# A new order table for a recurrent-attention and gated-MLP kernel: pairs loaded in natural order, weights at other places

## The chip, the cores and the metric

The kernel runs on one core of one Trainium2 chip. The metric is the device time in microseconds (us) of one execution; lower is better. The engines are PE (matrix products; PEld loads its weights), DVE, ACT and POOL (elementwise work), and SP, which here only issues transfers between memory and the chip.

## The reference

Two steps, on float32 inputs with batch 4, 8 heads, 768 positions, head size 48, model width 384, and 1024 hidden columns:

```python
for t in range(S):                       # gated linear attention, per batch and head
    state = alpha[:, :, t, :, None] * state + outer(k[:, :, t], v[:, :, t])
    y[:, :, t] = q[:, :, t] @ state
x = y, heads side by side                # [4, 768, 384]
h = maximum(x @ w_in, 0)                 # [4, 768, 1024]
u, v = h[..., :512], h[..., 512:]
v_n = (v - mean(v)) / sqrt(var(v) + 1e-6)
v_s = w_spatial @ v_n + b_spatial[:, None]   # mixes positions, [768, 768]
out = (u * v_s) @ w_out                  # [4, 768, 384]
```

## The kernel before

The 768 positions of each batch are cut into six chunks of 128; the 24 chunks are numbered through. Chunks 0 to 9 are worked as five pairs (`pair(j)`), the other fourteen singly (`single(i)`).

For a pair or a chunk, the work runs like this. Four loads (`ac`, `kc`, `qc`, `vc`; 384 KB each for a pair, 192 KB for a chunk, named `acs` and so on). A logarithm of alpha (`ln`, ACT). Its running sums (`cum`, `tot`, PE). Exponentials of the sums with both signs (`einv`, `eexp`, `ebc`, ACT). Products that give the scaled keys and queries (`kt` on POOL or DVE, `qt` on DVE) and a bfloat16 copy of v (`vb`). Transposes on PE (`tr`, `trk`) whose two halves are copied out of the matrix banks into `kqT` by `ev` or `evs`, each on DVE or ACT. Scores (`sc`, PE), masked on DVE (`m`, `ms`). The state update (`upd` on PE, `z` on DVE, `S` on POOL or DVE, the bfloat16 copy `sb`). The output of the chunk (`ya`, `y`, PE) and its copy `xe` into xT.

For each batch follow the projections: `v` per chunk (three matmuls of 512 columns), its copy with a maximum (`ve`), statistics (`bn`), an inverse deviation (`rs`) and the normalised `vn`; `u` per quarter of the hidden columns and half of the positions (three matmuls of 384 columns, copy `ue`); the spatial mix `s` in two parts, the first over the chunks 0 to 3 and the second over 4 and 5, with `se` (adds the bias) and `g` (multiplies by u); the output `o`, its copy `oe` and its store `st`. The spatial weights come in three loads (`w_sp`), are cast, transposed on PE (`wt`) and copied (`we`). `w_in` comes in two loads, `w_out` in one; the six weight loads share two buffers (`raw`), so that a weight load waits for the casts of the one before the last.

The order of everything is written out by hand in the string `PLAN`. A word such as `P94@7` is operation 94, issued on PE, into bank 7; D is DVE, A is ACT, G is POOL, S is SP. The operation numbers come from the order in which the Python code creates the operations. `replay` goes through the words and issues one after the other, so the words of one letter are the order of that engine's queue, and each engine works its queue strictly in that order:

```python
        for x in junk:
            cols, n = x.split("#")
            ...
            warm(int(cols), int(n))
        ...
        op.emit(eng)
```

A word may carry junk: `:512#0` calls `warm` ahead of the operation, a float32 matmul of 512 columns on the tile `junk` into bank 0, whose result nobody reads. `junk` is filled by operation 0 (`zeros`, DVE).

Line numbers used below: 268 `warm`; 431 the loads of pairs; 796 the weight loads; 210, 212 the copies on ACT and the other engines; 216, 218 the copies with a maximum; 221 products of two operands; 384 `z`; 452, 460 running sums; 518, 696 transposes; 543, 712 updates; 561, 724 scores; 569, 729 masks; 584, 740 chunk outputs; 754 all projections; 816, 817 statistics; 833 `vn`; 889 `se`; 920 stores.

Of the kernel before, what the change touches and what calls it, by code (L numbers as in the profile page):

```python
# [41 lines left out]
S53 D2 S103 D0 G8 G4 A57 P59@0:512#0:512#0:184#0 A107 A62 P58@1 D3
P51@2 P108@3:100#3 S54 P109@4 D1 A63 A60 S55 G5 A114 A61 A64
S162 A110 P49@5 D50 G6 D68 D65 A111 D66 D69 A166 P71@6,7:384#6
P74@5,1:144#5 A72 S56 G70 S105 P167@0:100#0 S104 A67 D73 D52 A112 D75
P168@7 P77@2,5 D78 A76 A113 P84@6,1:76#6 S163 S164 A169 A171 S106 G79
D116 S268 D86 G118 A80 P87@2,3:88#2 D85 A170 D119 G115 D89 D88
P124@1,6:236#1 P121@4,3:164#4 D81 D122 P90@2,5:52#2 A126 A125 D123 G177 S165 A172 D174
# [8 lines left out]
G281 D160 D285 P216@0 D282 A153 P212@1 P201@6 D161 A19 A205 A149
P214@3 P34@4,2 G284 D206 D211 G21 A217 A213 A202 D35 S23 P31@7,0
D33 P290@1,5 D101 A36 A32 P37@6,4 A38 P287@2,0 D39 D203 D289 G286
P154@7 A283 A215 G22 S319 D288 A207 D208 S322 P226@4 P218@6 P293@3,0  # L60
D209 A292 D294 D291 A155 P40@2,5 A42 P227 S320 P219 P222@7 G24
P223 A25 G295 S321 P46@3,5 A41 D228 A47 D220 A323 D224 P43@1,4
P230@2 A45 D297 P300@6,7 G221 P303@3,0 G229 S379 G334 A44 D48 P325@5
P231 P324@4 P234@1 D301 P238@6 G298 D304 G225 D326 S26 P239 A331
A327 A329 P242@3 P243 P235 A330 D305 G332 A328 D232 P246@0 G335
D302 D336 S403 D244 D333 A337 D240 P247 G296 P338@2,7 A339 G299
P341@5,3 A340 D236 P306@4,6 A383 S405 P308 P344@1,2 D342 D343 G233 S380
G245 S404 A307 S381 S546 G28 P351@5,7 A309 A30 D248 P354@3,0 P310@4
S382 G27 P313@6 G29 D345 D352 G346 P384@1 D356 A407 A311 D353
P408@5 G237 D355 P256@0 A385 S406 A347 P250@4 A314 D312 S513 D315  # L70
S489 P357@7,3 P358 S547 A409 S548 S490 S492 A386 G249 A359 P360
A410 P253@6 D348 D412 D254 G411 G388 A251 P365@7 A361 P362@2 A316
P373@4 A363 D389 G241 P391@5,3 P414@6,2 D257 S515 A366 A550 S491 P369@0
A374 G349 S611 A416 D364 G390 A392 S514 A370 A387 S516 P371@7
P259@4 D393 A517 D415 S635 P394@3 P398@6,2 S570 P417@5,0 D375 P265@1 D395
P518@3 G413 S549 G396 D399 A260 P262@6 G397 D419 A493 D418 A519
P367@4 S636 D400 D318 P420@0 G350 P401@5 P494@2 A263 D421 A376 A266
P551@6 D317 A495 D402 P425@1 A520 P422@0 A426 D377 S571 P435@5 S572
D378 S612 A521 A552 A423 D368 P433@1 S613 A553 P439@4 G498 A372
S637 S573 D427 D424 A500 A428 A436 P447@0 P443@7 G555 D523 S721  # L80
S614 S638 A497 G522 P437@3 D429 A434 D430 P504@5 D556 A496 D505
G506 P444 P448 A554 D499 P440 A438 D449 D445 P451@1 P452 D453
G507 P501@6,5 A524 D502 D441 P558@3,2 P525@0,7 P459@1 D526 P460 A503 G446
D559 P528@6 P431@5 S722 P508@4,0 G454 A527 G450 D560 A432 D529 A574
P565@7,3 P532@2,6 D461 P455@5 D567 P575@1 G442 P467@3 G557 A615 S778 G530
S723 P468 D566 D533 P474@7 A639 S745 D509 A576 D510 D534 A577
P616@2 A531 P561@4 P456 D562 P463@0 P640@6 D580 A617 P464 D457 P477@4
D469 A475 G579 D465 A618 G620 A641 G643 P582@7,5 S724 A578 D621
A584 P511@1 D583 P568@3 A642 S746 P535@0 A512 A478 A619 P471@5 D644
P537@7 P589@1,4 D569 G462 S748 A536 D472 P646@6,2 A538 D590 A581 S747  # L90
P623@0,3 D539 D648 P540@5 A647 D625 G563 S843 A624 P594@7 G458 P603@1
P585@6 A725 D591 A541 A622 G466 A595 P649@0,2 D586 G564 G470 P630@3,5
S780 P592@4 A604 G587 P726@6 S802 P626@7 D650 D542 S779 A593 S867
P486@1 D632 A727 P605@0 P480@4 A728 S845 G588 A487 D627 P599@5 S781
A782 G645 D631 A481 G730 S844 A543 D731 D651 A729 P483@1 D596
A606 G628 P733@7,3 D607 S803 A749 S869 G629 P633@4 D544 P652@6 D732
A634 P783@2 A653 A600 A608 P601@0 P597@4 P654@6 P736@5 A484 P750@1 A734
A655 S804 D735 D610 A751 A752 A786 S868 P667@3 D545 P657@7 P663@6
G754 A658 D737 D609 A598 P671@5 D656 P699@7 D602 A784 D659 A668
A847 P683@0 P679@4 D756 S805 P760@3 A660 D662 D661 A664 D755 P675@6  # L100
G738 A785 P684 A806 S846 A753 S261 D761 P672 S252 D788 P665@3
P676 D673 P680 P700 G787 D685 G686 P790@1,2 A666 P740@5,3 D677 D681
A871 P757@0,6 P848@4 G762 A791 S258 D741 A758 D792 P687@1 A759 G763
A789 A851 P797@5,0 P764@2,6 D742 P695@3 D701 G674 P669@7 A849 D765 D799
G852 P688 G678 P807@2 S870 D798 P691@0 A850 P872@5 G682 D670 D766
P696 A808 P793@7 P692 P706@6 S479 A873 S482 A810 A739 A809 A874
S473 D794 D697 S488 P703@7 A707 P767@3 G811 D853 G795 A704 D812
P800@4 D876 P743@6 G875 A768 A801 P855@2,7 S705 D693 P814@5,3 D689 D856
A744 G813 P878@0,4 P769@6 P817@1 P772@2 A815 A816 D698 A879 P821@5,3 D880
G702 D818 A796 D857 P881@4,0 G854 G819 A770 S476 P862@1,7 D823 D864  # L110
D822 P835@6 A773 P858@3 G694 D882 P709@2 D859 A877 P831@7 G820 D863
P829@5 A836 A710 P826@4 D883 D771 G860 P833@6 A827 P824@2 G690 A861
D828 P865@3 A825 A866 P884@1 P837@4 D834 P886@0 D830 A885 D774 A838
P899@2 P897@3 S255 A775 P889@1 A887 P901@6 D839 D776 D777 A840 D832
D841 A890 P715@4 D842 P718@5 D891 A716 D888 P895@0 P903@7 D902 P712@1
P907@4 A900 P919@2 S708 A892 D894 P911@6 D898 D893 P904 P912 D905
D906 P915@3 S485 A713 P916 S267 P908 D917 D909 P927@1 G918 D913
P920 A719 A896 D910 P923@5 P924 P931@0 D914 P928 P932 D925 D921
D929 S717 D922 S720 P940@7 D933 P934@3 P937@4 G926 D930 A941 P946@6
P952@5 A947 S714 S711 D935 P943@2 P949@1 S264 D938 A944 A950 D953  # L120
# [871 lines left out]
```

## Time and profile before

| | |
|---|---|
| Median of 3 runs | 147.65 us (147.55 to 148.86) |
| Span of the profiled execution, first to last instruction | 145.2 us |
| Mean granted PE clock | 0.983 |
| PE busy | 135.1 us (93%), 2243 matmuls, 38 of them junk (12.7 us) |
| DVE busy | 123.5 us (85%) |
| ACT busy | 103.4 us (71%) |
| POOL busy | 79.7 us (55%) |
| Loaded and stored | 23.60 MB and 4.72 MB |

Of the profiled execution the profile gives the span, not the device time around it; the median of the runs is 2.45 us above the span. Busy time counts an instruction from its start to its end, and on PE neighbouring matmuls overlap and their ends are modelled, so a busy PE may still be waiting between operations. On ACT and DVE an instruction's record is about 0.1 us longer than the distance to the next start.

### The profile page before, as it was taken

The page shows a single profiled execution, that of the slowest core. Times are in us where ns is not written, and L with a number is a line of the kernel's source. Part 1 is how long each engine was busy: PE and PEld are TensorE (multiplying, and loading weights), DVE is VectorE, ACT ScalarE, POOL GpSimd, SP SyncE. Part 2 cuts the span into 40 slices and gives each one's busy share as a digit, 9 for nine tenths or more (in the row PEclk, how much of TensorE's full clock was granted, in tenths as well). Part 3 has the DMA queues.
Part 4 walks back from the last instruction along what each step waited for, and adds up shares of the span by engine and source line. Part 5 has one row for each costly group of instructions (what it writes and reads, how often), then busy time and mean ns, then how long its engine had stood idle before and what let it go on. Part 6 is the DMA issues. An engine that isn't in the chain of part 4 may idle for free.

```text
span 145.2 us, 5523 instructions
## 1 busy us (share of the span) xinstructions
PE 135.1 (93%) x2243; PEld 83.1 (57%) x2243; DVE 123.5 (85%) x284; ACT 103.4 (71%) x262; POOL 79.7 (55%) x120
## 2 busy tenths in 40 slices
PE   5979899489999999999999999999999999999990
PEld 2447576344565665656556665665666766555560
DVE  5047999577999999799999998999799999997970
ACT  3579627817997669899895889999876996653031
POOL 6301944559325999954549789644369984000500
PEclk9999999977999999999999999999999999999997
DMA  4999999995799999977989999999999990015045
GB/s 116 267 261 261 266 237 276 287 320 117 227 305 264 282 188 187 184 156 145 197 171 194 182 171 178 210 167 204 190 152 237 317 362 14 5 56 209 8 146 181
DMA packets 84841, 28.66 MB, mean 197 GB/s; under 512 B 79568, under 2 KB 83280, under 8 KB 84816
## 3 DMA queue, kind: packets, MB, share of 16 engines
q1 hardware_dynamic: 84784, 28.32, 88.0%
q8 instruction: 17, 0.28, 0.9%
q14 instruction: 8, 0.07, 0.2%
q0 software_dynamic: 32, 0.00, 0.0%
HBM read 23.60 MB, written 4.72 MB: 195 GB/s over the span
## 4 chain that ended last, share of the span: by engine, by line
PE 71%; DVE 21%; issue 5%; ACT 0%; ACTq 0%; DVEq 0%
PE bank L754 45%; PE bank L268 5%; DVE stats L816 3%; DVE ptm L569 3%; DVE vn L833 2%; DVE ptm L729 2%; DVE qt L221 2%; PE bank L696 2%; PE bank L724 2%; PE bank L406 2%; PE bank L663 2%; PE bank L452 2%; PE bank L584 2%; PE bank L740 2%; DVE kqT L212 1%
## 5 line engine op out<-in xcount | busy, mean ns | idle before, releaser
L754 PE MATMUL bank<-w_spT,vn 128*128 128x384 bf16 x192 | 35.6, 326 | 0.3 <-DVE vn L833 0.2
L221 POOL TENSOR_TENSOR gT<-vs,uT 128x384 bf16<-128x384 f32 x25 | 22.5, 914 | 16.8 <-DVE vs L889 16.8
L221 POOL TENSOR_TENSOR kt<-kc,binv 128x384 bf16<-128x384 f32 x21 | 19.3, 930 | 10.8 <-ACT binv L673 8.7
L754 PEld LDWEIGHTS <-vn 128*128 128x128 bf16 x192 | 17.7, 97 | 12.3 <-DVE vn L833 1.2
L221 POOL TENSOR_TENSOR state<-zs,bc 128x384 f32<-128x384 f32 x20 | 16.7, 834 | 14.0 <-DVE zs L384 10.4
L754 PE MATMUL bank<-w_in,xT 128*128 128x512 bf16 x72 | 19.8, 406 | 0.0
L754 PE MATMUL bank<-xT,w_in 128*128 128x384 bf16 x96 | 19.4, 326 | 0.0
L754 PE MATMUL bank<-w_out_sb,gT 128*128 128x384 bf16 (+1 forms) x100 | 18.4, 320 | 0.1
L729 DVE TENSOR_TENSOR ptm<-bank,mask 128x512 bf16<-128x512 f32 x28 | 17.9, 681 | 0.4 <-PE bank L724 0.4
L216 ACT ACTIVATE v_sb<-bank 128x512 bf16<-128x512 f32 x23 | 13.7, 609 | 5.4 <-PE bank L754 5.3
L816 DVE BATCH_NORM_STATS2 stats<-v_sb 128x6 f32<-128x512 bf16 x24 | 16.4, 682 | 1.3 <-ACT v_sb L216 0.8
L889 DVE TENSOR_TENSOR vs<-bank,bsp_bc 128x384 f32<-128x384 f32 x31 | 15.9, 548 | 1.0 <-PE bank L754 0.8
L268 PE MATMUL bank<-junk 128*128 128x512 f32 (+16 forms) x38 | 12.7, 429 | 2.5 <-DVE junk L311 1.8
L210 ACT COPY kqT<-bank 128x512 bf16<-128x512 bf16 x22 | 12.1, 603 | 3.3 <-PE bank L518 1.7
L221 DVE TENSOR_TENSOR qt<-qc,bank 128x384 bf16<-128x384 f32 x24 | 12.7, 545 | 0.8 <-ACT bank L675 0.8
L569 DVE TENSOR_TENSOR ptm<-bank,mask 128x512 bf16<-128x512 f32 x20 | 13.0, 682 | 0.2 <-PE bank L561 0.2
L754 PEld LDWEIGHTS <-gT 128*128 128x128 bf16 x100 | 9.2, 98 | 5.9 <-issue 0.3
L754 PEld LDWEIGHTS <-w_in 128*128 128x128 bf16 x96 | 8.8, 97 | 6.6
L216 ACT ACTIVATE uT<-bank 128x384 bf16<-128x384 f32 x22 | 10.7, 499 | 2.0 <-PE bank L754 2.0
L833 DVE TENSOR_SCALAR vn<-v_sb,mvs,rstd 128x512 bf16<-128x512 bf16 x24 | 10.6, 466 | 1.3 <-ACT rstd L827 1.1
L268 PEld LDWEIGHTS bank<-junk 128*128 128x128 f32 x38 | 6.6, 210 | 8.8 <-issue 5.2
L384 DVE TENSOR_TENSOR zs<-bank,state 128x384 f32<-128x384 f32 x16 | 8.8, 550 | 2.8 <-PE bank L543 2.5
(110 smaller groups left out, 251.7 us busy)
## 6 DMA issues: line engine op xcount, KB each, us to landing
ac<-in_alpha_dram SPq DMA_DIRECT2D x14, 192.0 KB, 4.8
qc<-in_q_dram SPq DMA_DIRECT2D x14, 192.0 KB, 4.8
kc<-in_k_dram SPq DMA_DIRECT2D x14, 192.0 KB, 5.0
vc<-in_v_dram SPq DMA_DIRECT2D x14, 192.0 KB, 4.4
raw_w<-in_moe_w_spatial_dram SPq DMA_DIRECT2D x3, 768.0 KB, 4.5
out_dram<-raw_w SPq DMA_DIRECT2D x11, 192.0 KB, 3.0
ac<-in_alpha_dram SPq DMA_DIRECT2D x5, 384.0 KB, 5.4
kc<-in_k_dram SPq DMA_DIRECT2D x5, 384.0 KB, 6.3
```

The lines of the kernel that those rows point to most:

```text
L210: nc.scalar.copy(out=out, in_=in_)
L216: nc.scalar.activation(out=out, in_=in_, func=AF.Relu)
L221: ENG[eng].tensor_tensor(out=out, in0=in0, in1=in1, op=ALU.mult)
L268: nc.tensor.matmul(out=banks[n][:, 0:cols].rearrange("p (a b) -> p a b", a=4), lhsT=junk, rhs=junk[:, None, 0:cols // 4].to_broadcast([128 ...
L384: nc.vector.tensor_tensor(out=zs[i % 3], in0=tp(), in1=state[(i - 1) % 3], op=ALU.add)
L406: nc.tensor.matmul(out=place(y, n) if q(hp).shape == place(y, n).shape else place(y, n).rearrange("p (a t) -> p a t", a=2), lhsT=sbd[(i - ...
L569: nc.vector.tensor_tensor(out=ptm[n2][:, par, s], in0=banks[sl.bank].rearrange("p (hp t) -> p hp t", hp=HP), in1=mask[:, par][:, None, :]. ...
L729: nc.vector.tensor_tensor(out=ptm[n2][:, ci, s], in0=banks[sl_p[s].bank].rearrange("p (hp t) -> p hp t", hp=HP), in1=mask[:, 2][:, None, : ...
L754: nc.tensor.matmul(out=ps, lhsT=lhsT, rhs=rhs, start=first and n == 0, stop=last and n == len(pairs) - 1)
L816: nc.vector.bn_stats(out=stats[tt % 2], in_=v_sb[n2][:, tt, :])
L833: nc.vector.tensor_scalar(out=vn[n2][:, x, :], in0=v_sb[n2][:, x, :], scalar1=mvs[n2][:, x, 0:1], scalar2=rstd[n2][:, x:x + 1], op0=ALU.su ...
L889: nc.vector.tensor_tensor(out=vs[d], in0=banks[sl.bank][:, 0:TH], in1=bsp_bc[:, th, :], op=ALU.add)
```

## The change

Only the string `PLAN` differs. All 955 operations, their inputs and outputs and the rules of what waits for what are the same. The new table moves nearly every operation on every queue, gives some operations to another engine, other banks to PE's results, and other junk.

The loads on SP stand like this (before, then after, up to the first single chunk):

```
ac_0 ac_1 kc_0 qc_0 ac_2 vc_0 qc_1 kc_1 kc_2 qc_2 vc_1 ac_3 vc_2 w_in_1 w_in_0 qc_3 w_sp_0 kc_3 w_sp_1 vc_3 w_sp_2 ac_4 vc_4 kc_4 qc_4 acs_10 w_out

ac_0 qc_0 vc_0 kc_0 ac_2 ac_1 vc_1 kc_1 qc_1 w_in_1 qc_2 kc_2 w_in_0 vc_2 w_sp_0 ac_3 w_sp_1 w_sp_2 ac_4 qc_3 kc_3 w_out qc_4 vc_3 kc_4 acs_10 vc_4
```

Operations that change engine, net, where it is more than one: `ev` and `evs` copies 16 from DVE to ACT; `ue` 4 and `oe` 2 from DVE to ACT; `g` 4 and `S` 3 from POOL to DVE; `ve` 2 from ACT to DVE; casts of weights 4 to DVE (three from POOL, one from ACT) and 3 from ACT to POOL; `sb` 3 to DVE, and `vb`, `vbs` 3 from ACT to POOL. Junk goes from 19 calls with 3340 columns, the last ahead of operation 97, to 9 calls with 3664 columns, the last ahead of operation 134.

The first third of both tables:

```diff
-S53 D2 S103 D0 G8 G4 A57 P59@0:512#0:512#0:184#0 A107 A62 P58@1 D3
-P51@2 P108@3:100#3 S54 P109@4 D1 A63 A60 S55 G5 A114 A61 A64
-S162 A110 P49@5 D50 G6 D68 D65 A111 D66 D69 A166 P71@6,7:384#6
-P74@5,1:144#5 A72 S56 G70 S105 P167@0:100#0 S104 A67 D73 D52 A112 D75
-P168@7 P77@2,5 D78 A76 A113 P84@6,1:76#6 S163 S164 A169 A171 S106 G79
-D116 S268 D86 G118 A80 P87@2,3:88#2 D85 A170 D119 G115 D89 D88
-P124@1,6:236#1 P121@4,3:164#4 D81 D122 P90@2,5:52#2 A126 A125 D123 G177 S165 A172 D174
-D178 P92 P137@6,1 G82 P134@4,3 G117 A91 G120 A173 D175 D138 D136
-P180@2,7:108#2 P183@0,6:112#0 D184 A272 P127@3,0:56#3 A185 D135 A179 A93 D128 D139 S9
-G129 D181 P273@4:136#4 P274@3 A83 D182 P193@1,6:104#1 G130 D131 P190@2,7 G132 D194
-S13 A176 P140@0,5:80#0 G7 D275 A11 A12 P143 P141 G10 A133 D195
-A276 D192 P186@1 S270 P97@6:192#6 S17 A144 D187 P94@7 G188 G16 P156@1
 ...
+S53 D0 G4 A57 P58@0:512#0:472#0 A60 D1 A61 G5 G8 S55 D2 G6 D66 P59@1 A62 A63 D69 P74@0,2:512#2:272#2 A76 D3 S56 D70
+S54 D75 P51@3 S162 G67 G68 D65 P71@2,0:360#4 A73 D72 P87@0,2:280#4 D89 A166 P167@4 P84@5,6 S103 P77@2,7 S106 S104 A64
+A107 P108@1 A110 A169 S105 D78 G120 G79 G7 D85 D88 D86 P109@2 A114 A111 A52 A112 A170 A113 G118 D115 P49@5
+P121@3,6:512#0:512#0 D81 A117 P127@7,0 D116 D119 D80 G82 S9 P124@2,1 A126 A122 A125 D128 D129 D131 P168@7 A171 A123
+A172 A173 P90@3,1 S164 S163 D175 P134@6,2:232#0 A91 G11 G12 D178 D135 D136 G10 G132 G174 G177 P92 P183@4,0 P137@3,7
+D138 D139 A93 G133 P94@1 A185 G83 A95 P97@2 S13 S165 P180@1,3 G16 A181 A182 P140@7,0 P141 A130 D184 D96 D15 D50
+P193@3,1 D194 D195 P190@4,6 G14 D192 D191 A142 A98 D99 G176 A179 P145@7 P143 A144 A146 S17 P186@1 P150@3 P156@6 P148@4
+G18 D187 D188 D157 A151 A100 D147 D158 D101 A19 S268 S20 G189 P196@3,7 P152@1 P197 P154@0 P199 A198 P201@3 D202 D102
+P31@6,2 A153 G21 G22 A200 P216@7 P34@1,5 P214@3 D36 P204@5 A33 D217 D203 S23 D35 S319 A155 A272 A159 A149 D161 D32
+D160 A205 P37@7,0 P212@2 A38 P273@1 P40@5,4 P274@6 A39 P226@0 P222@7 D206 G24 G25 D275 A276 A42 A213 A207 D208 P218@2
 ...
```

Some of the numbers: 57 to 64 logarithm, sums and exponentials of pair 0; 71, 74 the transposes `tr_k_0`, `tr_q_0`; 77 `upd_0`; 84, 87 its scores; 90 `ya_0`; 94, 97, 145, 156, 201, 204 the six `v` of batch 0; 121, 124, 134, 137 transposes and scores of pair 1; 122, 123, 125, 126 the `ev` copies of pair 1; 180, 183, 186 transposes and update of pair 2; 196 `ya_2`; 208, 209 the last `vn` of batch 0; 218 to 247 the `s` of batch 0; 31 to 46 `wt` and `we`; 9, 13 `w_in`; 17, 20, 23 `w_sp`; 26 `w_out`.

More of the change, by code (lines that the diff above doesn't have):

```diff
@@ L41 @@
 PLAN = """
[L42 to L48, printed above, removed]
@@ L57 @@
[L57 to L64, printed above, removed]
@@ L65 @@
[L65 to L120, printed above, removed]
@@ new lines @@
+D209 P223 D224 P219 D220 A277 A41 P46@5,4 S270 P227 D228 A323 A278 D282 P324@7 A215 A47 P43@3,2 A279 D285 D44 A48 A45
+P230@5 P325@1 P231 P210@2 A327 P290@3,4 A211 P246@0 P242@2 P247 S269 D281 D326 D284 D232 S26 S321 S271 D29 D292 P243
+P287@4,5 A291 A328 A329 A28 A331 G221 G229 G233 D30 G225 D27 D244 D333 P238@3 P239 P256@2 D248 A330 D336 D240 S320
+A289 A280 A288 P303@4,0 A257 A286 D304 P300@6,7 S379 G249 D302 D305 S322 P250@1 A251 P341@4,3 A342 A343 A383 G283
+P293@2,5 D294 D301 G332 D295 P234@1 P235 G335 P338@2,3 A340 G296 S403 D236 S381 S380 P306@6,0 P384@4 A339 P308 S382
@@ new lines @@
+S404 S405 D245 D297 P351@2,3 P354@1,7 D309 D352 D356 A385 A337 G241 A307 G334 P253@5 P344@6,0 P310@2 A254 A407 P408@7
+P313@5 G298 G299 A386 G237 D355 D345 D353 P262@6 G346 A409 P357@3,1 P358 D389 D347 P360 A311 A387 D348 G388 P391@0,4
+A314 A410 D312 D392 D315 D412 S489 S514 S406 S513 S546 S491 S490 S492 S516 P265@5 G349 D350 A359 A361 P373@0 A390
+P394@1 P371@3 A393 P398@7,4 A374 A266 G411 D395 G396 G413 G397 S570 P414@0,2 P259@1 P362@5 A415 A416 P417@2,0 S515
+S611 D400 D375 D399 D418 D419 A263 A316 P365@6 A493 A363 S548 S549 S572 S547 D318 D317 D364 D372 D366 P369@7 P494@2
@@ new lines @@
+P401@5 P420@0 S571 A497 A402 P367@4 P422@5 A421 A370 A376 P425@7 A423 D377 D378 D424 A517 A426 P433@6 A434 A495 P443@5
+A368 G498 G500 D427 A428 A496 D260 D430 A524 P447@7 P431@6 P518@4 P451@3 P435@1 P439@0 A519 A520 A432 D429 D499 P448
+D449 P444 D445 P452 P504@6 A436 P440 A550 D453 D441 D454 P551@7 A552 P501@5,1 D505 G522 D450 D523 A503 P528@3 G446
+G442 G506 P437@2 P467@0 A521 A502 A574 A438 P468 D469 P459@6 P575@4 D529 G470 G557 G530 P508@2,5 P525@0,1 A553 A576
+A507 A615 A577 A526 A578 A554 G555 D509 P463@3 P455@2 P456 P464 D527 D556 D580 D510 D465 P477@0 A478 D457 P460 D461
@@ new lines @@
+P616@5 S573 S612 S613 G579 G462 A617 A618 G458 G620 G581 G466 P532@3,7 P558@2,0 G531 D534 D533 D560 S635 P582@4,1 A583
+P471@6 A472 A559 A619 P474@7 P561@0 P511@6 P535@3 A475 D584 D621 D562 A536 P565@5,2 P589@1,4 P623@7,0 S636 P540@3 A639
+D512 D590 D567 P640@1 S637 A624 A625 D566 D591 G563 A641 A642 P486@7 P537@0 A564 S745 S614 P568@5 P592@4 S721 S638
+G643 A541 D644 P646@3,1 P630@2,6 D569 A487 A593 A538 A647 P585@7 P597@4 P594@0 S724 S746 S747 S778 S802 S722 A648 S723
+A749 S843 S804 G622 S779 S748 S780 S803 S867 S844 P480@3 P626@1 D542 D586 G587 D539 D632 D627 A598 A481 A588 P750@7
@@ new lines @@
+A753 A725 D631 P649@6,4 P605@3 A606 G628 G629 G645 P601@1 P603@2 D650 D651 P726@6 P633@4 P652@3 D607 A543 A595 D596
+D653 A634 P599@0 A732 A604 A727 A728 A608 D544 P654@4 P483@2 D655 D545 P657@3 D610 D600 D609 P665@4 A729 A658 A751
+A752 A602 A666 A806 D659 D656 D755 A660 D661 A847 A484 G730 G754 P663@5 P679@0 P675@3 P671@1 P667@4 P683@7 D662 P676
+D731 P680 A664 A782 P736@6 P684 P672 D677 D681 G682 D737 D668 D685 P687@3 P807@6 A808 P688 D673 P783@4 P757@7,0
+P733@5,2 P695@1 P696 A809 A784 D812 D759 D674 D689 A810 A785 A735 D788 D697 G678 G738 G686 P669@0 P699@6 A734 A758
@@ new lines @@
+G739 G787 G756 S845 P700 D701 A670 A786 P848@5 S781 S868 P740@7,3 D742 S805 S869 P790@0,1 A849 A791 D741 A871 A792
+A850 P764@4,2 G702 P691@6 P692 G811 P706@7 D765 D766 P760@4 D761 D690 G698 A851 P872@1 A873 A707 P703@0 A704 D693 D853
+P743@4 P767@2 P814@7,3 A744 P797@6,0 G852 G762 G763 G875 D799 D789 D798 D694 A816 A815 P769@4 A770 A768 P709@3 P793@7
+P855@4,0 A857 A874 P821@6,5 D794 D822 G813 A710 A856 D876 D823 P772@2 P715@0 P817@3 P878@6,7 G795 A796 D818 S846 G854
+G819 G820 A879 P800@4 P824@5 P862@6,3 D880 D825 P881@7,1 D864 D883 A801 P712@4 S488 S485 D713 P826@5 P858@3 D859 G860
@@ new lines @@
+P833@1 A834 S870 A877 G861 P837@4 P718@3 P829@1 D882 D863 A838 A773 D771 A827 D774 P884@4 P865@2 P835@5 D839 D828
+P831@6 A866 A836 A885 A775 D777 D776 A840 P886@2 P899@4 A900 A887 D841 P889@5 D842 D888 S267 S708 S476 S479 S261 S473
+S714 A832 A890 A719 S720 D891 A892 D893 S258 S705 S711 P897@7 A898 P911@4 P919@6 A716 S252 S482 S264 D894 P927@5
+P903@3 P907@2 D830 S717 P908 P904 D909 D905 D906 P931@1 P912 P915@0 P916 P928 S255 D913 P923@4 D914 D917 G910 P924
+P932 P901@0 A902 D929 D925 G926 P895@4 P920 A896 D918 D921 G922 P940@0 P937@4 A941 S942 P934@6 A938 S939 A935 S936
@@ L122 @@
+D930 D933 P952@1 D953 P949@4 S954 P946@0 A947 D950 S951 S948 P943@4 A944 S945
 """
```

12 lines of the change are left out of this document (4 added, 8 removed).

## The prediction

> **What bounds it now.** I read the page first, for which engine is full where.
>
> ```profile
> PE 135.1 (93%) x2243; PEld 83.1 (57%) x2243; DVE 123.5 (85%) x284; ACT 103.4 (71%) x262; POOL 79.7 (55%) x120
> ...
> PE   5979899489999999999999999999999999999990
> ...
> DVE  5047999577999999799999998999799999997970
> ...
> DMA  4999999995799999977989999999999990015045
> ...
> q8 instruction: 17, 0.28, 0.9%
> ```
>
> PE and DVE are both full from about the tenth slice on. The DMA row is full from the second slice to the ninth: the start is set by loads. Next, the busy time by stretches.
>
> ```profile
> 12.00:16.00 4.00, 3.81 (x70) 2.73 (x68) 3.08 (x8) 3.47 (x9) 2.06 (x3) 1.00 1.28 263
> ...
> 28.00:32.00 4.00, 2.52 (x10) 1.16 (x10) 2.21 (x4) 1.47 (x4) 1.50 (x3) 0.88 0.91 289
> 32.00:40.00 8.00, 8.00 (x120) 4.14 (x119) 6.57 (x16) 6.51 (x18) 5.29 (x8) 0.85 0.67 175
> ...
> 40.00:130.00 90.00, 89.71 (x1567) 55.82 (x1565) 86.22 (x190) 74.22 (x195) 58.27 (x76) 1.00 0.94 190
> ```
>
> The columns are length, busy PE, PEld, DVE, ACT, POOL, then clock, DMA share, GB/s. Up to 28 us much of PE's busy time is L268 (the `warm` matmuls, 12.7 us of the 135.1). From 40 to 130 us DVE is busy 86.2 of 90 us (96%), ACT 82%. The timeline shows what separates the two stages.
>
> ```profile
> 26.50 0.47 PE L543 MATMUL bank<-vb,kt 64*128 64x96 bf16 x7
> ...
> 29.48 0.20 PE L543 MATMUL bank<-vb,kt 64*128 64x96 bf16 x1 [2.51 <-issue]
> ...
> 30.04 4.36 PE L754 MATMUL bank<-w_in,xT 128*128 128x512 bf16 x12
> ```
>
> In the middle of one update PE stands for 2.51 us and waits for nothing the profile names. The trace's packet records show a 16 KB packet of the instruction queue (q8) starting at 26.98 us and taking 1.10 us; I read the gap as PE out of instructions. Behind it the clock is halved for 3.41 us (31.02 to 34.43; 0.88 and 0.85 above), and twelve projection matmuls take 4.36 us.
>
> What lies ahead of 30 us is mostly not work. I summed, over PE's operations, the distance from start to start that each kind shows where PE runs dense (u 0.49, v 0.65, s 0.65 and 0.325, o 0.65, ya 0.67, tr 0.3, sc 0.25). All operations together are 112.6 us; only 9.9 us of them start before 30.0. The other 102.7 take the 111.5 us to 141.5, a rate of 0.92. The same sum for DVE (0.46 for a 384-column operation, 0.60 for a masked score, 0.81 for a statistics pair, 0.32 to 0.33 for vn and kqT) gives 117.4 us, more than PE's.
>
> **The change.** Nothing is computed more or less. Counting the letters, DVE goes from 242 to 237 operations, ACT 233 to 244, POOL 105 to 99. The prices come from these groups.
>
> ```profile
> L221 DVE TENSOR_TENSOR qt<-qc,bank 128x384 bf16<-128x384 f32 x24 | 12.7, 545 | 0.8 <-ACT bank L675 0.8
> L212 DVE COPY kqT<-bank 128x512 bf16<-128x512 bf16 x26 | 10.0, 412 | 0.0
> ...
> L210 ACT COPY kqT<-bank 128x512 bf16<-128x512 bf16 x22 | 12.1, 603 | 3.3 <-PE bank L518 1.7 <-PE bank L696 1.5
> L216 ACT ACTIVATE uT<-bank 128x384 bf16<-128x384 f32 x22 | 10.7, 499 | 2.0 <-PE bank L754 2.0
> ```
>
> DVE gives 16 net kqT copies to ACT (-6.6 us at 0.412) and 4 ue (-2.2), 2 oe (-1.1), and takes 4 net g (+2.2), 3 S (+1.7, priced as the 0.55 of a 384-column operation), 4 casts (+1.8), 2 ve (+1.4), and 3 sb, xe, kt, vb against vbs and be (about +1.8). That is -1.0 us of busy time. ACT gains 16 x 0.603 + 4 x 0.499 and loses casts, vb, sb and ve: about +5 us. POOL loses some 5 us, of no worth, since it is busy 65% from 40 to 130 us. Junk falls from 19 to 9 calls, 3340 to 3664 columns, all within the first 21 us; it costs nothing while PE waits for loads.
>
> Now the start under the new order. `D0` stands first, so junk may start near 1.0 us (now 1.79), and 984 columns end at 4.7, before the first logarithm ends at 5.22; the first cumulative sum moves from 5.98 to 5.3. Loads set the rest: the first nine land 1.50 us apart, from 4.4 to 16.4 us (393 KB at 263 GB/s). In the new SP order these are all of pair 0, ac_2, and all of pair 1; w_in (loads ten and thirteen) then lands near 20.5 and 26.4, kc_2 near 23.7, vc_2 near 27.9, the first w_spatial third near 30.3 (now 32.4).
>
> Following the engine orders with these landings and the row durations: tr_q_0 8.6, tr_k_0 10.1, sc_0 11.2. Then ACT's queue (ln_2, ln_1, the exponentials) sets the pace: the eexp_1_1 ends 17.5, tr_k_1 17.6, tr_q_1 18.6. All four ev copies of pair 1 are on ACT, with einv_2_1 between them: 4 x 0.58 + 0.5, so sc_1 starts at 21.9 (now 19.1, with two on DVE). qc_2 and eexp_2_1 let tr_q_2 go at 23.3; v_0_0 and v_0_1 follow at 23.9 to 25.2 (now 30.0), tr_k_2 25.4, sc_2 27.1, upd_2 29.2, and from 29.6 PE has u and v work without a gap. DVE ends pair 2's masks at 30.9, as now (30.94). At that point PE has done four v and two u that it now does later.
>
> The next marker is the last vn of batch 0, which gates the second half of every s. DVE has 10.1 us of steps from 30.9 to it: 41.6, against 44.9 now, 3.3 us earlier. But the new table has put only 26.7 us of DVE's steps ahead of that marker where the old had 28.7, so 2.0 us of DVE work is put off. At DVE's pace of 0.95 (79.9 busy of 83.5 us from 44.9 to 128.4) this costs 2.1 us: net -1.2 us if DVE sets the rest. For PE the comparison stands at the first second-half s: 41.6 against 44.66, with 0.7 us of work put off: net -2.3 us if PE sets the rest. Both engines are within 6% of full, so I take the middle, -1.75.
>
> The end: the last store is a whole 192 KB tile (o_3_3, oe_21) instead of a half one; oe_21 took 0.48 against 0.33 us, its landing 1.91 against 1.76: +0.3. Loads of pairs 3 and 4 come later (kc_3 near 41.9, now 33.7; w_out waits for two POOL casts, near 44.3), behind w_sp_2, which waits on SP for a cast on ACT at 33.0. PE reaches tr_k_3 near 48 and o_0_2 near 49, so the s of batch 0 hides them; without that cover each would cost its 1.5 us transfer. The sum is -1.75 + 0.3 = -1.45 us, span 143.75. The profiled span is 145.2; the median of the runs is 147.65, so 2.45 us lie around it, taken as unchanged: 146.2.
>
> Clock: my pass leaves PE with only some 1.3 us of matmuls between 20.3 and 23.7 us. The trace's one halving ahead of the end followed a stretch with 2.5 us of idle PE. [...] Unknown cost of a halving near 24 us: from 0 (PE waits for copies anyway) to 1.7 us (half of 3.41, as dense work); I take 0, since the waits around it are about 1.5 us.
>
> [...]
>
> **Rivals.** (1) PE sets the rest: all of -2.3 is kept, +0.3 for the end, 145.6. For it: PE's dense rate. Against: DVE's 96%. (2) Slower: ACT becomes the bound. In the new table both kqT halves are on ACT in 14 of 24 transposes (now 4), so the second half comes 0.6 us later before its scores. Ten more such places x 0.6 = 6 us of lateness; if two thirds meet a waiting PE, +4 against -1.45 gives 150.2. It decides once ACT is busy over 88 of 90 us, or PE's waits on kqT pass 1.5 us. For it: 74.2 + 5 us of ACT in 90, in-order. Against: six or more PE operations stand between most transposes and their scores. (3) The start is lost: the fetch stall comes back (2.5 us) or the clock halves (1.7): -1.45 + 2 = 148.2. (4) The table does nothing measurable, because DVE's put-off work eats the lead: 147.5; this is the edge of the forecast with DVE at 0.93.
>
> **How the numbers follow.** Forecast (lead kept in part, 146.2, own range 144.9 to 147.4) 0.40; (1) 0.20; (2) 0.24; (3) 0.10; (4) 0.06. A difference of 1%, 1.5 us, is about what a measurement of this kernel can tell from none. Faster by over 1% (below 146.17): half of the forecast and all of (1), 0.40. Slower (above 149.13): nearly all of (2) and a third of (3), 0.25. The rest, 0.35, is within 1%. Range: from 143.6, with PE's lead and 2 us more out of DVE's idle 4%, to 150.2, with ACT as bound.
>
> **What would show it.** Right: the first v matmuls (L754) near 24 us, PE without a gap above 1 us after 28 us, no clock below 1.00 between 28 and 40 us, the last vn (L833) of batch 0 near 41.6, DVE busy about 96% after 45 us. Wrong: PE waiting for kqT copies (L210) by more than 1.5 us, ACT above 88 of 90 us, an "issue" gap of over 1 us, or the vn marker after 44 us.

## The result, and the profile after

The new table takes 152.76 us (median of four runs, 152.22 to 153.89) against 147.60 for the old one on the same chip: a ratio of 1.039 with a 95% interval of 1.0286 to 1.0494. The forecast was 146.2. A ratio, here and in the table of experiments, leaves out each kernel's runs over 1.5% above its fastest, so it can differ from the ratio of the medians. The profiled execution is the slowest of the four, 153.89 us, with a span of 152.1; 1.8 us lie around it. All line numbers of the new kernel are 34 lower than those of the old one (L754 is L720, L221 is L187, L210 is L176, L216 is L182), because the table takes fewer lines.

First the page of the new kernel, which answers to the page shown in the prediction.

```profile
PE 137.9 (91%) x2223; PEld 81.0 (53%) x2223; DVE 126.4 (83%) x279; ACT 110.0 (72%) x273; POOL 76.8 (50%) x114
...
PE   7898888899789999999996799999999899999990
...
DVE  5154979899769999999986589999999999998850
...
q8 instruction: 17, 0.28, 0.8%
```

No engine is full through the middle any more. PE and DVE have dips at the same two places: the eleventh and twelfth slices (38 to 46 us) and the twenty-second and twenty-third (80 to 87 us). Where two engines have a dip together, it is worth looking whether one waits for the other. The stretches (length, busy PE, PEld, DVE, ACT, POOL, then clock, DMA share, GB/s):

```profile
28.00:32.00 4.00, 3.87 (x68) 2.00 (x64) 3.47 (x7) 3.01 (x7) 0.83 (x1) 1.00 0.74 217
32.00:40.00 8.00, 8.00 (x172) 4.16 (x172) 7.79 (x19) 6.01 (x15) 3.79 (x5) 1.00 0.79 215
40.00:130.00 90.00, 84.09 (x1423) 51.68 (x1421) 82.77 (x170) 73.06 (x190) 51.95 (x67) 1.00 0.91 173
```

The start did what was forecast: the clock is 1.00 where it was 0.88 and 0.85, and between 32 and 40 us PE issues 172 matmuls where it issued 120. The loss is in the 90 us behind it: PE is busy 84.1 us instead of 89.7, DVE 82.8 instead of 86.2, and ACT 73.1 instead of 74.2.

By the sum of work of the prediction (112.6 us of PE operations in all) PE has started 19.6 us of work by 40 us, against 18.2 before; at 50 us 27.4 against 26.9; at 65 us 38.6 against 40.5; at 80 us 53.0 against 54.9; at 95 us 63.7 against 68.9. So the lead is there, it is gone by 55 us, and 3.3 us are lost between 80 and 95.

Two places stand out. The first, on ACT, DVE and PE (the columns are start, length, engine, line, what it does, and in brackets the idle time before it and what ended it):

```profile
40.89 0.49 ACT L444 ACTIVATE binv<-bank 128x384 bf16<-128x384 f32 x1 [1.68 <-DVE bank L434]
41.28 0.47 ACT L176 COPY w_spT<-bank 128x384 bf16<-128x384 bf16 x1
41.64 0.51 ACT L182 ACTIVATE uT<-bank 128x384 bf16<-128x384 f32 x1
42.02 0.31 ACT L792 ACTIVATE rstd<-mvs,eps_tile 128x2 f32<-128x2 f32 x1
```

```profile
40.32 0.54 DVE L434 TENSOR_TENSOR bank<-bank,la 128x384 f32<-128x384 f32 x1
42.59 0.74 DVE L799 TENSOR_SCALAR vn<-v_sb,mvs,rstd 128x512 bf16<-128x512 bf16 x2 [1.74 <-ACT rstd L793]
```

```profile
42.20 1.85 PE L720 MATMUL bank<-w_spT,vn 128*128 128x384 bf16 x8 [1.32 <-ACT uT L182]
```

ACT stands 1.68 us at `einv_3_0` until DVE has added the sums of pair 3 (`c1_3`). `einv_3_0` has no use for that result: it needs only `cum_3_0`, which PE ended at 38.99 us. But both read the bank of `cum_3_0`, and `c1_3` stands ahead in the table. Behind it in ACT's queue are a copy of weights, `ue_0_1_1` (which frees bank 2 for `s_0_0_0_0` on PE, 1.32 us of waiting) and `rs_0_4`. DVE then stands 1.74 us for that `rs_0_4`. Neither of the two chains needs the other: only the order of the queues ties them.

The second place, on ACT, DVE and PE:

```profile
81.09 0.35 ACT L646 ACTIVATE bc<-bank 64x4 f32<-64x4 f32 x2 [1.70 <-DVE qt L187]
81.47 0.58 ACT L176 COPY kqT<-bank 128x512 bf16<-128x512 bf16 x1
81.95 0.53 ACT L620 ACTIVATE la<-ac 128x384 bf16<-128x384 f32 x1
```

```profile
80.51 0.54 DVE L187 TENSOR_TENSOR qt<-qc,bank 128x384 bf16<-128x384 f32 x1
...
85.98 1.02 DVE L187 TENSOR_TENSOR qt<-qc,bank 128x384 bf16<-128x384 f32 x2 [1.57 <-ACT bc L646]
```

```profile
82.53 0.32 PE L629 MATMUL bank<-la,le_one 128*128 128x384 bf16 x1 [1.47 <-ACT la L620]
...
87.66 0.32 PE L629 MATMUL bank<-la,le_one 128*128 128x384 bf16 x1 [1.09 <-DVE ptm L695]
```

`ebc_13` (the `bc` of chunk 13, an exponential of four columns that `cums_13` left in a bank) waits on ACT for `qts_13` on DVE, and has no use for its result. Both read the same bank. The trace shows the one that stands later in the table starting when the other has ended (`ebc_13` 0.04 us after the end of `qts_13`, as `einv_3_0` 0.03 us after that of `c1_3`), and `qts_13` stands eight words ahead of `ebc_13`. While ACT waits, `lns_15` is queued behind it, and PE's `cums_15` waits for that. Five microseconds later it is the other way round: `qts_14` on DVE waits 1.57 us for `ebc_14` on ACT, though `eexps_14`, whose result it needs, ended at 83.23; `ms_12_1` is behind it on DVE and `cums_16` on PE waits for the bank that `ms_12_1` frees. So at both places it is a pair of readers of one bank that stands crosswise.

### The profile page after: what moved, and what is told of

Its sections match the earlier page's. It is cut to its first block, busy times and chain, and to the rows that moved or that the text cites. A ratio compares the mean times of both kernels' runs of the same rounds, so it can differ in the third digit from the quotient of the medians.

```text
span 152.1 us, 5490 instructions
## 1 busy us (share of the span) xinstructions
PE 137.9 (91%) x2223; PEld 81.0 (53%) x2223; DVE 126.4 (83%) x279; ACT 110.0 (72%) x273; POOL 76.8 (50%) x114
## 4 chain that ended last, share of the span: by engine, by line
PE 52%; DVE 24%; ACT 7%; DMA 5%; issue 5%; POOL 4%; DVEq 0%; POOLq 0%; ACTq 0%
PE bank L720 35%; DVE vs L855 3%; DMA vc<-in_v_dram 3%; DMA ac<-in_alpha_dram 2%; PE bank L234 2%; DVE ptm L535 2%; DVE ptm L695 2%; PE bank L690 2%; DVE qt L187 2%; DVE stats L782 2%; PE bank L706 2%; ACT kqT L176 2%; PE bank L418 2%; DVE gT L187 2%; PE bank L662 2%
## 5 line engine op out<-in xcount | busy, mean ns | idle before, releaser
L720 PE MATMUL bank<-w_spT,vn 128*128 128x384 bf16 x192 | 35.8, 327 | 1.4 <-ACT uT L182 1.3
L187 POOL TENSOR_TENSOR gT<-vs,uT 128x384 bf16<-128x384 f32 x21 | 20.1, 965 | 30.6 <-DVE vs L855 23.0
L176 ACT COPY kqT<-bank 128x512 bf16<-128x512 bf16 x38 | 21.3, 591 | 6.5 <-PE bank L484 4.2
L720 PEld LDWEIGHTS <-vn 128*128 128x128 bf16 x192 | 17.3, 97 | 13.4 <-issue 1.7
L187 POOL TENSOR_TENSOR kt<-kc,binv 128x384 bf16<-128x384 f32 x20 | 18.1, 912 | 11.3 <-ACT binv L639 10.1
L720 PE MATMUL bank<-xT,w_in 128*128 128x384 bf16 x96 | 20.2, 328 | 0.0
L187 POOL TENSOR_TENSOR state<-zs,bc 128x384 f32<-128x384 f32 x17 | 14.8, 869 | 10.2 <-DVE zs L350 8.9
L187 DVE TENSOR_TENSOR qt<-qc,bank 128x384 bf16<-128x384 f32 x24 | 12.9, 546 | 7.7 <-ACT bank L447 4.5
L720 PE MATMUL bank<-w_in,xT 128*128 128x512 bf16 x72 | 19.2, 380 | 0.0
L720 PE MATMUL bank<-w_out_sb,gT 128*128 128x384 bf16 (+1 forms) x100 | 18.7, 320 | 0.5 <-DVE vs L855 0.3
L182 ACT ACTIVATE uT<-bank 128x384 bf16<-128x384 f32 x26 | 12.6, 492 | 6.9 <-PE bank L720 6.8
L182 ACT ACTIVATE v_sb<-bank 128x512 bf16<-128x512 f32 x21 | 12.3, 596 | 1.8 <-PE bank L720 1.8
L720 PEld LDWEIGHTS <-gT 128*128 128x128 bf16 x100 | 9.0, 97 | 7.4 <-POOL gT L187 1.0
L234 PE MATMUL bank<-junk 128*128 128x512 f32 (+5 forms) x18 | 10.9, 728 | 1.3 <-DVE junk L277 1.1
L720 PEld LDWEIGHTS <-w_in 128*128 128x128 bf16 x96 | 8.3, 98 | 5.9
L178 POOL CAST vb<-vc 128x384 bf16<-128x384 f32 x14 | 7.2, 512 | 6.7 <-DMA vc<-in_v_dram 6.7
L176 ACT CAST xT<-bank 128x384 bf16<-128x384 f32 x19 | 8.8, 481 | 2.1 <-PE bank L372 1.9
```

What stands on the lines that cost most here:

```text
L176: nc.scalar.copy(out=out, in_=in_)
L178: ENG[eng].tensor_copy(out=out, in_=in_)
L182: nc.scalar.activation(out=out, in_=in_, func=AF.Relu)
L187: ENG[eng].tensor_tensor(out=out, in0=in0, in1=in1, op=ALU.mult)
L234: nc.tensor.matmul(out=banks[n][:, 0:cols].rearrange("p (a b) -> p a b", a=4), lhsT=junk, rhs=junk[:, None, 0:cols // 4].to_broadcast([128 ...
L720: nc.tensor.matmul(out=ps, lhsT=lhsT, rhs=rhs, start=first and n == 0, stop=last and n == len(pairs) - 1)
```

## The experiments

The times, each against runs of the old kernel on the same chip. The old kernel's medians in these comparisons lie between 147.48 and 148.18 us, so kernels of different comparisons are set side by side by their medians.

| Kernel | Median, us | Ratio to the old kernel (95%) |
|---|---|---|
| new start, old rest | 152.23 | 1.030 (1.024 to 1.035) |
| old start, new rest | 157.46 | 1.060 (1.051 to 1.070) |
| copies on the old engines | 156.86 | 1.062 (1.058 to 1.066) |
| other banks | 152.33 | 1.030 (1.025 to 1.035) |
| two ebc first | 150.78 | 1.026 (1.014 to 1.038) |
| einv_3_0 later | 151.16 | 1.034 (1.025 to 1.042) |
| the three words together | 148.82 | 1.016 (1.009 to 1.023) |
| qc_3, kc_3 before the third w_spatial | 152.63 | 1.044 (1.035 to 1.053) |
| three words, two g on POOL | 148.99 | 1.010 (1.006 to 1.014) |
| three words, all POOL work back | 153.31 | 1.033 (1.028 to 1.038) |
| three words, late POOL work back | 152.06 | 1.023 (1.018 to 1.029) |
| three words up to ya_3, then old | 146.95 | 0.993 (0.989 to 0.996) |
| three words up to y_10, then old | 149.50 | 1.010 (1.006 to 1.014) |
| old up to y_10, then three words | 155.85 | 1.047 (1.039 to 1.054) |
| three words up to cums_16, then old | 153.70 | 1.039 (1.034 to 1.044) |
| old, one word crossed | 148.68 | 0.999 (0.993 to 1.004) |

The new kernel itself, in the same manner, is 152.76 and 1.039.

**Start and rest apart.** Two kernels cut both tables at `vn_0_4`, near 42 us.

```diff
 (new start, old rest)
+ the new table up to vn_0_4, then what is left in the old table's order (13 banks differ)
 (old start, new rest)
+ the old table up to vn_0_4, then what is left in the new table's order (6 banks differ)
```

> The first 211 words of the new table (up to the fifth vn of batch 0, some 42 us), then the remaining operations in the order of the old table; 13 banks differ. Theory R (the rest of the new order loses, by waits of PE for banks that DVE and ACT empty late; the start is as good as predicted): 145.0 to 147.0 us, because at 40 us the new run had started 1.4 us more of PE's work than the old. Rival L (the new start itself loses, because the loads of pairs 3 and 4 and w_out come late): 150 us or more, with PE gaps on tr_k_3, upd_3 and the first o.

> The reverse: the old table up to the fifth vn of batch 0, then the rest in the new order; 6 banks differ. Theory R: as slow as the new kernel or slower, 152.5 to 156 us. Rival L: back at 147 to 149 us.

Both are slow, 152.23 and 157.46. In the first PE loses its lead at the seam (20.2 us of work at 40 us, but 23.2 at 50): the old rest wants pair 3 first, whose loads and products come later in the new start, and PE stands 2.74 us ahead of `tr_q_3`:

```profile
44.31 0.41 PE L492 MATMUL bank<-ident,qt 64*128 64x64 bf16 x16 [2.74 <-DVE qt L195]
```

Behind this gap the profile shows the clock halved for 6.83 us, from 45.40 (all four runs have a mean clock of 0.973 to 0.977). So the seam costs twice, by the wait and by the clock, and from about 60 us on the kernel runs at the old pace. For this mix the rival L (pair 3 is late) holds. The second is even slower than theory R had it; in it both holes of the new rest are there again, behind the old start:

```profile
85.73 0.32 PE L637 MATMUL bank<-la,le_one 128*128 128x384 bf16 x1 [1.48 <-ACT la L628]
...
90.86 0.32 PE L637 MATMUL bank<-la,le_one 128*128 128x384 bf16 x1 [1.08 <-DVE ptm L703]
```

(In kernels whose table is broken into shorter lines, as this one, all line numbers are 8 above those of the new kernel.) These waits of 1.48 and 1.08 us are the 1.47 and 1.09 of the new kernel: they belong to the order of the rest, not to its start. Part of this kernel's time is clock as well: its profile shows two stretches of 3.41 us at half clock, from 31.15 and from 55.04 us.

**The copies.** All `ev` and `evs` copies back on the engines of the old table, the order untouched.

```diff
-A73 D72 ... A122 ... A123 ... A181 A182
+D73 A72 ... D122 ... D123 ... D181 D182
```

> The new table, but every ev and evs copy on the engine that it had before (16 net go back from ACT to DVE). Rival C (ACT carries too many kqT copies, PE waits for them): 149 to 150.5 us. Theory R (it is the order in the queues): within 1.5 us of the new kernel, 151.5 to 154 us, since DVE gets 6.6 us more to do.

156.86 us, slower than either theory had it and 4.1 us slower than the new kernel, with ACT at only 66.8 of the 90 us. In this order the copies on ACT are not what costs; taking them away makes it worse.

```profile
40.00:130.00 90.00, 81.60 (x1403) 49.51 (x1402) 82.75 (x176) 66.79 (x175) 50.77 (x65) 1.00 0.89 170
```

DVE got 16 copies more and is busy for the same 82.75 us (82.77 in the new kernel). So DVE is not full either: in both it waits the rest of the time.

**The banks.** 206 operations get, of the banks that are free at their word, the one that the trace shows free first.

```diff
-P74@0,2 ... P51@3 ... P71@2,0 ... P87@0,2
+P74@2,3 ... P51@4 ... P71@5,6 ... P87@7,0
```

> The new table in the same order and on the same engines, but each result of PE goes into the free bank whose last reader ended first in the profile of the new kernel (206 operations change bank). Rival B (the choice of bank makes PE wait, other banks were free): the 10 us of bank waits mostly go, 147 to 149 us. Theory R (the readers are late as such, in queues that wait in turn): within 1.5 us of the new kernel, 151.3 to 154 us.

152.33 us, as theory R had it: 0.4 better, within the spread. PE stands 1.48 us ahead of `cums_15` (1.47 in the new kernel), since it waits for ACT and not for a bank.

**The crossed words.** Three kernels move words within ACT's queue and nothing else (521 and 554 are `ebc_13` and `ebc_14`, 276 is `einv_3_0`, 213 `ue_0_1_1`, 207 `rs_0_4`).

```diff
 (two ebc first)
-A519 A520 A432 ... P467@0 A521 A502 A574 ... A553 A576 ... A578 A554
+A519 A520 A521 A432 ... P467@0 A502 A574 ... A553 A554 A576 ... A578
 (einv_3_0 later)
-A276 A42 A213 A207 D208
+A42 A213 A207 A276 D208
```

> The new table with two words moved on ACT's queue: ebc_13 and ebc_14 directly behind eexps_13 and eexps_14, ahead of evs_12_1 and evs_13_0. Nothing else changes. Theory X (queues that stand crosswise): ebc and qts read the same bank and are kept in the table's order; in the new table ebc_13 waits 1.70 us on ACT for qts_13, which holds back lns_15 and cums_15 (PE 1.46 us idle at 81.05), and qts_14 waits 1.57 us on DVE for ebc_14, which holds bank 5 and cums_16 (PE 1.1 us idle at 86.57). With the two words moved both holes go: PE's cums_15 follows s_1_1_1_0 within 0.3 us, cums_16 follows s_1_1_1_1 within 0.4 us, and the time falls by 2 to 3 us to 149.8-150.9. Rival D (the rest of the new order is simply dense on DVE and ACT, and these holes are where the lateness happens to show): the lateness comes back at the next scores, 152.0-153.5.

> The new table with one word moved on ACT's queue: einv_3_0 behind we_3_1, ue_0_1_1 and rs_0_4 instead of ahead of them. Theory X: einv_3_0 waits 1.7 us for c1_3 on DVE with three copies queued behind it, so bank 2 (ue_0_1_1) comes free late and s_0_0_0_0 starts 1.3 us late, and rs_0_4 and with it the last vn of batch 0 come 1.5 us late. With the word moved s_0_0_0_0 starts by 41.1 instead of 42.20, the last vn ends by 42.0 instead of 43.33, the time falls by 1.0 to 1.4 us to 151.2-152.0. Rival L (pair 3's late loads set the pace here: kc_3 lands at 43.3, vc_3 at 48.5): the vn is earlier, but tr_k_3 and upd_3 are not, and the time stays at 152.3-153.2.

> The three words of the two experiments together. Theory X: the gains add, 148.4-149.8, one to two per cent above the kernel before. Rivals D and L: 151.5-153.

The two `ebc` bring 2.0 us (150.78), `einv_3_0` 1.6 us (151.16), both together 3.9 us (148.82; the single gains add up to 3.6). All six runs of the three words together (148.29 to 149.29) lie below all runs of the new kernel (from 152.22). All three came out as theory X said, the second 0.04 us better than the edge of its range; its rivals L and D are out for these 3.9 us. The profile of the three words together, ACT and PE at the second place:

```profile
77.46 0.52 ACT L649 ACTIVATE bank<-bank 128x384 f32<-128x384 f32 x1
78.01 0.36 ACT L654 ACTIVATE bc<-bank 64x4 f32<-64x4 f32 x2
```

```profile
77.89 0.34 PE L637 MATMUL bank<-la,le_one 128*128 128x384 bf16 x1
...
82.08 0.32 PE L637 MATMUL bank<-la,le_one 128*128 128x384 bf16 x1 [0.16 <-DVE ptm L703]
```

The `bc` of chunk 14 follows its exponential at once, `cums_15` starts without a wait and `cums_16` after 0.16 us. At the first place `rs_0_4` now runs at 38.6, ahead of `einv_3_0`, and the last `vn` of batch 0 ends at 39.9 us instead of 43.3. From 40 to 130 us all engines are busy for more of the time:

```profile
40.00:130.00 90.00, 87.11 (x1486) 54.15 (x1495) 86.43 (x178) 75.98 (x196) 52.74 (x68) 1.00 0.90 171
```

**The loads of pair 3.** Both loads ahead of the third load of w_spatial (`S23`).

```diff
-D203 S23 ... S270 ... S269
+D203 S270 S269 S23
```

> The new table with qc_3 and kc_3 moved on SP's queue ahead of the third w_spatial load (w_sp_2), which in the new table waits on SP for a cast; all else as in the new table. Theory L (pair 3's late loads cost): kc_3 lands 5 us earlier (38 instead of 43.3), w_sp_2 3 us later (40.6 instead of 37.6); pair 3's transposes come earlier, 151-152. Theory X: pair 3's keys were not what PE waited for, and the later w_sp_2 holds back wt_5 and the second half of the positions, 152.7-154.5.

152.63 us, no different from the new kernel (theory X had 152.7 or more). `kc_3` is issued at 27.6 us instead of 34.8, and nothing follows from it: `tr_k_3` starts 5.49 us behind `wt_5` in both. The s of batch 0 hide these loads in the new order, as the prediction said. Theory L is out for pair 3.

**POOL's work.** The new table has moved products from POOL to DVE. Two of them took more than twice their usual time of 0.55 us there (the three-word kernel, DVE; POOL beside the second one):

```profile
107.38 1.28 DVE L195 TENSOR_TENSOR gT<-vs,uT 128x384 bf16<-128x384 f32 x1
...
113.41 1.33 DVE L195 TENSOR_TENSOR gT<-vs,uT 128x384 bf16<-128x384 f32 x1
```

```profile
113.40 0.92 POOL L195 TENSOR_TENSOR kt<-kc,binv 128x384 bf16<-128x384 f32 x1
114.28 1.16 POOL L195 TENSOR_TENSOR state<-zs,bc 128x384 f32<-128x384 f32 x1
```

```diff
 (two g on POOL; 674 and 690 are g_2_0_0 and g_2_0_1, 678 g_2_1_0, 787 and 852 kts_20 and kts_22)
-D674 ... G678 ... G787 ... D690 ... G852
+G678 G674 G787 ... G852 G690
 (late POOL work back, on top of that)
-D295 ... D245 ... D350 ... D454 ... D450 ... D694
+G295 ... G245 ... G350 ... G454 ... G450 ... G694
 (all POOL work back: these and ten more of S, kt, vb, g and casts)
```

> The new table with the three words of the experiment before moved, and besides g_2_0_0 and g_2_0_1 on POOL as in the old table (with g_2_1_0 ahead and kts_20 behind g_2_0_0, g_2_0_1 behind kts_22). Theory P (a DVE product whose two inputs both lie in SBUF is held up by POOL's work): these two products took 1.28 and 1.33 us on DVE against 0.55 of the same product where POOL stands, so DVE gets back 2.6 us in the stretch 105 to 120 us where the chain of DVE's scores (sc_20 0.68 us late behind se_2_1_1) holds PE back; PE's waits there fall from 2.3 to about 1 us, time 147.3-148.1 (against 148.82 with the three words alone). Rival Q (it is the queues' order again, not the price of these two): POOL gets 1.8 us more in front of kts_20 to kts_22, and the time stays at 148.4-149.4.

> As the run with two g on POOL, and of the others only S_6, g_0_2_1, sb_9, g_1_2_0, g_1_3_0 and g_2_1_1 back on POOL, at the places where their words stand. Theory P: DVE gets 3.2 us back, 146.3-147.5. Rival Q: se_1_3_1 on DVE waits for g_1_3_0 (one buffer), which POOL reaches only behind kts_13, and the time is 148-150.

> As the run with two g on POOL, and the other 16 operations that the new table took from POOL to DVE (S_2, S_4, S_6, four g, four casts and sums of weights and keys, vb_0_1, sb_9) back on POOL, at the places where their words stand. Theory P: DVE gets 8 us of its queue back, 146.0-147.6. Rival Q (POOL's queue takes the lateness over, since the casts of w_out and kt_3 then stand in one row on it): 148.5-151.

148.99, 152.06 and 153.31 us, against 148.82: rival Q in all three, and worse than it said in two. The stretched products are real, but two of them back on POOL gain nothing: a third, `g_2_1_1`, then takes 1.13 us on DVE instead of 0.54. More of them back cost 3 to 4.5 us. With the late ones back `kts_13` stands behind `g_1_3_0` on POOL, which takes 0.91 us for each, and PE stands 1.54 us ahead of `upd_13` for it; what makes up the rest of the loss was not traced further.

**The rest, cut at other places.** In the three-word kernel PE leads the old one by 2.4 us of work at 55 us, by 1.3 at 65 and by 0.8 at 80, and is 1.6 us behind at 130.

```diff
 (up to ya_3, near 53 us; no bank differs)
+ three-word table up to ya_3, then what is left in the old order
 (up to y_10, near 66 us; no bank differs)
+ three-word table up to y_10, then what is left in the old order
 (old up to y_10; three banks differ)
+ old table up to y_10, then what is left in the three-word order
 (up to cums_16, near 82 us; one bank differs)
+ three-word table up to cums_16, then what is left in the old order
```

> The new table with its three words moved, up to ya_3 (52.8 us); from there the old table's order for what is left, no bank changed. In the trace of the three-word run PE has done 2.4 us more work at 52 us than before, and 1.5 us less at 130. Theory T (that lead is real and the rest of the new order loses 4 us of it by itself): the old rest keeps most of the lead, 144.6-146.4. Rival S (a rest only runs at its pace behind its own start; whatever is late at the seam costs the lead, as at the seam of the first experiment, where 3 us went at 40 to 50): 147.5-150.

> The same with the seam at y_10 (66.2 us, where the three-word run leads by 1.2 us of PE work). Theory T: 145.5-147. Rival S: 147.8-150.

> The reverse: the old table up to y_10 (68.4 us), then the rest of the new table with its three words moved; three banks changed. Theory T: the rest of the new order loses 2.5 us by itself, 149.5-151. Rival S (the new rest is as fast, only the start differs): 147.5-148.8.

> New with three words moved up to cums_16 (82.1 us, lead 0.5 us), then old; one bank changed. Theory T: 146.3-147.8. Rival S: 148-150.

The first takes 146.95 us, 0.993 (0.989 to 0.996) of the old kernel: the only version whose median lies below those of both tables. Theory T expected at most 146.4, rival S 147.5 or more; neither came. In its profiled execution the whole lead is lost between 50 and 60 us (28.6 us of work at 50, 1.7 ahead; 35.8 at 60, as before), and from 60 us on every PE operation starts within 0.13 us of its time in the trace of before. Both spans are 145.2 us. So these two traces don't show what the 1.1 us between the medians is made of.

```profile
40.00:130.00 90.00, 88.29 (x1508) 54.58 (x1507) 85.33 (x185) 75.05 (x196) 55.22 (x71) 1.00 0.92 181
```

The other three are slower than either theory said or as rival S said: 149.50, 155.85 and 153.70. They open new holes at the seam: PE stands 1.53 us ahead of `cums_13` for `ue_1_3_0` in the second, 2.19 us ahead of `upd_13` for `qts_13` in the third, and 0.84, 1.16 and 0.70 us ahead of `sc_14`, `o_1_1` and `y_12` in the fourth. Behind the holes of the third and the fourth the profiles show the clock halved again, for 3.41 us from 83.32 and for 6.83 us from 88.84. So they don't weigh the rest by itself. That the rest of the new order gives back some 4 us of PE's pace between 55 and 130 us is in the trace; which of its parts does it stays open (PE's waits of over 0.15 us behind 55 us add up to only 1.4 us there).

**One word crossed in the old table.** `ebc_15` (578) is moved to directly behind `qts_15` (580), ahead of four operations of ACT.

```diff
-D580 A617 ... A475 ... A618 ... A641 ... A578 D621
+D580 A578 A617 ... A475 ... A618 ... A641 ... D621
```

> The old table with one word moved on ACT's queue: ebc_15 from behind einvs_17 to directly behind qts_15's word, ahead of einvs_16, oe_7, eexps_16 and einvs_17. Theory X (ebc waits for the qts that stands ahead of it in the table, and ACT's queue waits with it): in the trace of before sb_13 on ACT ends at 82.39 and qts_15 on DVE at 84.60, so ACT stands for 2.2 us, einvs_16 starts 2.0 us and evs_15_1 0.9 us later, PE is held up behind them, and the one word costs 0.6 to 1.5 us: 148.7-149.6 against 148.1. Rival (a wait on an engine that is busy 8.5 of 10 us at that place is absorbed): 147.6-148.4.

The wait came as expected:

```profile
85.50 0.36 ACT L654 ACTIVATE bc<-bank 64x4 f32<-64x4 f32 x2 [2.25 <-DVE qt L195]
```

Laid beside the trace of before, the PE operations between 72 and 84 us start 0.86 us later there (from the start of that run), and nearly all from 85.2 us on 1.61 us later, and the span is 1.6 us longer: one word costs 0.75 us in the trace. The times don't resolve it: the medians are 148.68 against 147.48, but the ratio is 0.999 (0.993 to 1.004). Inconclusive as a time; as a mechanism it is seen.

## Why the prediction was wrong, step by step

- **What bounds it before, and the start of the new order.** Right from the first `v` on. The first `v` matmuls are at 24.17 us (forecast 23.9), the update of pair 2 is at 29.84 (29.2), pair 2's masks end at 30.98 (30.9), and the clock is 1.00 from 28 to 40 us. Ahead of that the forecast times were too early (`sc_0` came at 13.77, forecast 11.2), which was made up by the first `v`.
- **Fetch stall 0, clock cost 0.** The clock cost was 0, and the stall nearly. The sum has no term for a stall; that there would be none was the author's estimate, since the traces show when a packet of q8 runs and not when it is asked for. In the trace of before PE stood for 2.51 us at the 960th of its loads and matmuls; in the new kernel the 960th comes at 32.05 us in `ya_2` and has no gap. A shorter gap that the prediction left out stands some 260 loads and matmuls earlier, in `ya_1`, behind a 16 KB packet of q8 that runs from 24.63 to 25.87 us; I read it as the same kind of stall:

```profile
27.20 0.56 PE L550 MATMUL bank<-ptm,vb 64*32 64x128 bf16 x44 [0.84 <-issue]
```

  In the other profiles with this start the gap at this place is between nothing and 1.43 us.
- **The last vn at 41.6.** It ended at 43.33. This is the first step that failed: the pass counted DVE's 10.1 us from 30.9 to that marker (41.0 by this sum; the text goes on with 41.6) and took `rs_0_4` on ACT as ready. ACT stood 1.68 us at `einv_3_0` ahead of it. With that one word moved it ends at 40.45, and with all three moved at 39.91, earlier than forecast.
- **The rate of the rest, unchanged at 0.95 for DVE and 0.92 for PE.** This is the step that failed most, and with it the lead that the sum of -1.45 us rests on. The rest was taken as the old one with a lead in front, but its order is new as well, and in these runs the rate changed with the order alone: three words moved brought DVE from 82.77 to 86.43 of 90 us and PE from 84.09 to 87.11. In the new kernel DVE is busy 92% ("about 96%" was the sign), and PE has three gaps of over 1 us behind 28 us (1.32, 1.47 and 1.09), where none was forecast. What stood in place of an unchanged rate is two places where the queues of ACT and DVE wait crosswise, worth 3.9 us. Queue order was followed up to 31 us only; the two crossed `ebc` and `einv_3_0` were in the table to be read.
- **DVE 1.0 us less to do.** Mis-sized. The records of DVE's operations add up to 142.7 us against 140.9: 1.8 more. `g` was priced at 0.55 us on DVE; the eleven `g` there took 8.28 us, 0.75 each, and the four more of them cost 4.0 us instead of 2.2. In the traces of before and after, the DVE products of 384 columns that read or write a bank (`qt`, `se`, `z` and the like) took at most 0.57 us in all 96 cases with over 0.1 us of POOL's work beside them; the 14 with neither input in a bank took 0.55 to 1.32 us. In the rows shown above it is 1.28 and 1.33 us on DVE beside a busy POOL, and 1.16 for POOL's state product beside one of them where 0.83 is usual. But other `g` on DVE beside a busy POOL took 0.55 to 0.97 us, so a busy POOL alone does not say which product is stretched. The term decided nothing here: 148.99 with the two products back on POOL.
- **Loads of pairs 3 and 4 hidden.** Right for pair 3 (152.63 with two of its loads earlier); pair 4's were not moved.
- **2.45 us around the span.** Mis-sized by 0.65: in the runs of these kernels time and span differ by 1.8. The profiled execution of before, at 145.2, was one of its quicker ones.
- **The end, +0.3.** It did not come: from the end of PE's last matmul to the end of the span the traces show 3.55 us against 3.62 before.
- **Rival 2, ACT as the bound at 150.2.** The side was right and the cause was not: ACT is busy 73.06 of 90 us, not over 88, PE's weight loads wait 1.1 us in all for `kqT` copies (over 1.5 was the sign), and with the copies off ACT the kernel gets slower. That 152.76 lies beyond its 150.2 on the slow side is no support for it. **Rivals 1 and 4** did not come; of rival 3 only the short stall named above.

What settles most of it: 3.9 of the 5.2 us by which the new table's median is higher lie in three words of ACT's queue. By the ratios it is less of the whole: 1.044 for the kernel with two loads moved, which is no different from the new one, goes to 1.016 with the three words on the same chip. What stays open is the rest, 0.8 us of the medians between the three-word kernel (148.82) and the old one (148.03 in that comparison; 1.6% by the ratio), and with it where its lead of 2.4 us at 55 us goes.

## What to carry to other kernels

When a whole order is exchanged, follow every queue to its end, not only to where the start is over: look for an instruction that waits for another engine while that engine soon waits for something queued behind it. In this kernel readers of one bank on two engines were such pairs (waits of 1.68, 1.70 and 1.57 us) although no data passed between them; here it helped to put the one first that was ready first, or to let what stood behind the waiting one go ahead. And take two tables' halves together only after looking at the seam: of six mixtures here one came out no slower than both tables.
